# Two interleaved heads per band section instead of four, with a new order of all engines

## The chip, the cores and the metric

The kernel runs on one core of one Trainium2 chip. The metric is the device time of one execution in microseconds (us); the number to beat is the median of three executions, 129.38 us.

## The reference

Two independent layers read a sequence of 2048 positions and 448 features each, and their results stand side by side in the output (2048 x 896, bf16).

```python
# A: sliding attention, 16 heads of 28, window of 8 positions with a step of 2
qkv = (x @ wqkv).reshape(B, S, 3, H, Dh).transpose(2, 0, 3, 1, 4)
idx = pos[:, None] - (jnp.arange(8) * 2)[None, :]          # s, s-2, ..., s-14
logits = jnp.einsum("bhsd,bhswd->bhsw", q, k[:, :, idx]) * Dh ** -0.5   # idx < 0 is masked
o = jnp.einsum("bhsw,bhswd->bhsd", softmax(logits), v[:, :, idx])
a = o.transpose(0, 2, 1, 3).reshape(B, S, D) @ wo
# B: a diagonal complex recurrence of 448 states
h[t] = Lam_bar * h[t - 1] + B_bar @ x[t]
y[t] = 2 * Re(C @ h[t]) + x[t] * Dskip
```

## The kernel before, in words

**The order.** Every operation is a small function with a name, and the string `ORDER` lists the calls one by one. The position in that list is the order in which each engine receives its instructions; nothing is reordered later. A step such as `QK041@23` puts its result into PSUM banks 2 and 3; a trailing `.` lets ScalarE empty the bank and a trailing `=` lets VectorE do it. Each engine walks through its own part of the list and waits where an operand isn't ready, so a late step delays all that is behind it on the same engine.

**Layer A.** `QA`, `QK` and `V_` (lines 343 to 361 and 510 to 518) multiply x by wqkv on TensorE; `qk`, `qh` and `v` empty the banks. `P(u, r)` (line 402) is one VectorE multiplication of queries with eight shifted copies of the keys, 128 x 4096 elements; there are 14. Its result is a tile of a pool with three buffers, so the fourth `P` waits until the `E_` of the first has read it. `E_` (lines 415 and 419) sums the products over the 28 features of a head on TensorE, `lt`, `TR` and `tr` bring the logits to rows of positions, and `sma`, `smb`, `smc` are the softmax of one half u of the sequence (VectorE, ScalarE, VectorE).

The weighted sum over the window is a banded matrix product. `AL(g)` shifts the attention weights of four blocks of 64 positions into place, `al` writes them to a zeroed tile, `ad` copies that tile to DRAM, and `sp(g)` (line 505) reads it back so that each row arrives one position later than the row before it: the band `PT`. For each group of `HS` heads the band stores `HS` values of one position next to each other. `AV(B, hg, par)` (lines 531 and 537) then takes one head out of it as the moving operand, every `HS`-th element, 128 x 135 at a time; four heads run in four groups of 32 columns of the array. The lines that carry `HS`:

```python
PW = HS * (128 + 7)
SP.dma_start(late["PT"][32 * s:32 * s + 32, sl:sl + 4, :, 32 * HS * s:32 * HS * s + 39 * HS].rearrange("p t g n -> p (t g) n"),
             pd_ap(g, 32 * s * 2560, [[2560 - HS, 32], [40 * HS, 64 // HS], [1, 39 * HS]]))
PE.matmul(p[32 * hh:32 * hh + 32, 128 * bl:128 * bl + n], v_s[:, t, 4 * hg + hh, :],
          PT[:, t % NS, (4 * hg + hh) // HS, (4 * hg + hh) % HS:HS * n:HS], start=(bl == 0 and B == 0), stop=True, skip_group_check=True)
```

`AV(0, ...)` needs `sp(0)` and `sp(1)`, `AV(1, ...)` needs `sp(2)` and `sp(3)`; `sp(3)` overwrites the part of `PT` that `AV(0, ...)` reads. `av` empties the bank, `W_` multiplies by wo, `w` and `ow` bring the rows out.

**Layer B.** The recurrence is split into four phases j of 512 steps and seven groups g of 64 complex states. `BU` and `BR` build the inputs (banks emptied by `z`), `UP`, `y`, `sa`, `sb`, `sd` run the scan over 256 longer steps on VectorE (g in pairs 0, 2, 4 and 6), and `DN`, `dn` finish phase 3. The carried-in state must then be added, rotated, to phases 0 to 2 of every group: 21 rotations. A rotation goes one of two ways. `H_` and `h` (lines 790 and 795) do it as one TensorE matmul and one VectorE addition. `ha` and `hb`, or `ka` and `kb` (lines 819 and 823), do it as two VectorE instructions, once `sw(g)` has fetched a copy with the halves swapped. `C(j, ct)` multiplies the finished states of all seven groups by the output matrix, `c` adds the skip term on VectorE, `oc` writes the rows out. `CH` and `ch` are the last block in two parts.

Of the kernel before, what the change touches and what calls it, by code (L numbers as in the profile page):

```python
# [18 lines left out]
NC = S // T  # L19
N2 = NC // 2  # L20
G = 7
HS = 4
PW = HS * (128 + 7)
NS = 12
PI = math.pi
# [4 lines left out]


ORDER = """
WU@0 XI0@12 xi00. xi20= XI1@3 xi31. QA000@4 xi30= QA200@5 xi01= PP@6 pcopy pa xi21= pb QA10@7 pd_ XA11@0 XH1@1 xh1. pe
QA001 xa11= pc pf XA10@2 QA201 QA30@6 xa10= QA11@3 tf1 ts01 tf5 ts05 QA01@1 ts11 QK011 qk010. QK001 qk001. V_111@02
V_110 ts21 QA21@7 tz xt0 pg pk QA31@1 QK031 v111. QK021 qk011. QK041@23 ts15 qk021. rb2 qk031. ts25 qk020. QK040 tf0
qk041. P01 wc= qk040. rb0 qk000. qk030. QK050@71 v110. V_100@53 QK051 qk050. ts00 ts10 qk051. QK061@24 V_101 tf6
V_001@60 V_000 v101. QK060 ts20 QK110@71 ts06 ts16 xt2 v100. v000. ts26 P03 qh001. E_01@3 qh000. E_03 P05 E_05 qh010.
qh011. v001. tf3 QK100@56 P02 P00 QK101 qk100. ts03 QK111 qk110. V_011@24 qk111. qk101. V_010 v010. v011. QK130@05
QK131 V_401@71 QK121@62 P04 E_00@4 ts13 E_02 E_04 qk130. QK120 tf2 qk131. hc0 ts23 qk121. ts02 V_400 P06 v400. P10
E_06 v401. ts12 lt00 ts22 QK141@05 BD P11 V_511@27 lt01 qk120. QK140 TR0@1 xt3 xt1 V_510 tr0. qk141. E_11@4 tf4 P13  # L40
qk140. E_10@3 ts04 QK161@61 LC v510. v511. P12 QK151@50 QK150 qk150. ts14 qk151. QK160 qh100. P14 qh111. V_410@27 sma0
qh101. qh110. V_500@50 hc1 V_501 v500. V_411 v410. E_12 E_13 OZ BU201@61 v501. v411= BU301@52 BU200 P15 ts24 XR tx
smb0 BU300 z30. P16 z20. BU000@07 BR31 BR21 ci0. CD0 E_14 z31. z21. ci3. ci2. E_15 smc0 CD2 BU311@56 BU001 BU401@21
E_16 rb1 lt10 lt11 BU400 TR1@3 BU310 ci1. z40. xd2 z00. BU500@42 BR41 tr1. BR32 z32. AL0@0 BR01 CD1 al0. z01. CD3
BU010@35 BU011 BU501 z41. sma1 smb1 BU101@07 ad0 BR02 z02. BR33 z33. z50. rb3 BU100 OP pm0 z10. BU210@13 BR11 BU211
xd0 smc1 pm1 BU111@40 ca6 pm3 pm4 z11. wo BU110 BR12 ca3 BR22 z12. xd3 BR03 z22. AL1@7 cs6 BR13 AL2@4 cs3 al1. BR51
z03= sp0 UP0 BR23 xd1 z13. y0= UP1 z51. y1. sa0 AL3@1 al3. BU410@72 al2. z23. sb0 sd0 ad1 ca0 ad2 BU511@50 BU411
BU601@14 UP3 ca5 cs5 pm2 y3. BR42 sp1 UP2 z42. BU600 BU510 BR52 z60. z52. DN0@6 BU611@71 BR61 y2. cs0 BR53 z53. BR43
BU610 UP5 z43. UP4 ad3 z61. BR62 ca2 y5. sa2 AV030@5 AV010@3 av010. sp2 AV031@4 av031. AV020@0 AV000@3 AV011@4 y4.
av000. AV021@2 z62. AV001@3 av030. dn0 BR63 av020. sb2 sd2 H_20@6 sa4 W_00@7 z63. h20 sp3 W_10@5 sb4 UP6 W_30@0 av001.  # L50
av021. w00. av011. sd4 y6. DN2@3 ca4 cs4 dn2 H_11@6 W_01@2 w10. w30. ow00 W_21@7 H_01@4 DN4@1 w21. dn4 sw5 sa6 h11
W_31@5 W_11@0 H_00@7 w11. W_20@3 w31. cs2 h00 h01 sb6 ha15 H_21@1 AV111@0 AV130@5 ow11 ow10 AV101@6 w20. ow31 av111.
ow21 ca1 h21 cs1 AV131@3 sd6 sw4 AV121@0 AV120@7 av120. sw2 AV100@4 ha24 AV110@1 av100. av121. C33@7 DN6@4 dn6 av110.
av131. C31@0 ha23 av130. av101. W_60@1 W_70@3 ow30 ha22 sw3 hb15 ha26 hb24 ha25 w01. W_41@5 H_10@4 w70. C32@6 hb23
ow01 sw6 h10 W_71@2 C30@3 ha03 w60. ow60 hb25 H_12@1 W_50@4 w41. hb26 ow41 ow20 c30 W_61@5 w61. hb22 c33 ow70 ow61
ha13 ka04 ha14 W_51@3 w51. hb13 oc33 w71. ow71 hb14 w50. W_40@7 C21@5 h12 ha16 w40. hb03 C20@3 hb16 c20 c21 ow40 C22@2
oc21 H_02@4 c31 C10@7 c22 oc22 h02 C13@1 C23@3 ka06 oc30 oc31 oc20 kb04 ka05 c32 oc32 kb05 kb06 C12@5 ow50 C11@0 c11
c12 ow51 c13 c23 c10 oc11 oc12 oc13 C01@2 c01 C00@4 c00 oc23 oc10 C02@6 CH0@0 CH1@5 oc01 c02 oa00 oc02 ch0 oh0 ch1 oh1
"""

@with_exitstack
def kernel(
# [46 lines left out]
    def ps(dt=F32):  # L109
        return ps_p.tile([128, 512 if dt == F32 else 1024], dt, tag=f"ps{banks.pop(0)}", name="ps")  # L110

    def evict(e, o, i):
        (ACT.copy if e == "A" else V.tensor_copy)(o, i)  # L113
# [356 lines left out]
    def pd_ap(g, off, ap):  # L470
        p = pds[g][:]
        return bass.AP(p.tensor, p.offset + off, ap)

    @op
    def AL(g):
        p = pp["al", g] = ps()
        p4 = p.rearrange("p (t g w h) -> p t g w h", t=4, g=H // HS, w=W)

        def at(t0, n, cc):
            return attn[:, t0:t0 + n, cc:cc + H].rearrange("p t (g h) -> p t g h", h=HS)  # L480
        for w in range(W):
# [7 lines left out]
    def ak(g):  # L489
        return Ak0[:, g] if g < 2 else late["Ak"][g]  # L490

    @op
    def al(g, e):
        evict(e, ak(g).rearrange("p (s n) -> p s n", n=40 * HS)[:, :, 0:W * HS],
              pp.pop(("al", g)).rearrange("p (s n) -> p s n", n=W * HS))

# [5 lines left out]
    def sp(g):  # L502
        sl = (4 * g) % NS
        for s in range(4):
            SP.dma_start(late["PT"][32 * s:32 * s + 32, sl:sl + 4, :, 32 * HS * s:32 * HS * s + 39 * HS].rearrange("p t g n -> p (t g) n"),
                         pd_ap(g, 32 * s * 2560, [[2560 - HS, 32], [40 * HS, 64 // HS], [1, 39 * HS]]))
# [467 lines left out]
```

## Time and profile before

| | before |
|---|---|
| median of 3 runs | 129.38 us (129.23 to 130.12) |
| profiled execution | 130.03 us, its span in the profile 128.3 us |
| granted TensorE clock | 0.996 |
| TensorE matmul busy | 121.7 us (95%) |
| VectorE busy | 118.3 us (92%) |
| ScalarE busy | 90.2 us (70%) |
| DMA | 23.28 MB in 44916 packets |

The profile comes from one execution, which took 130.03 us, 0.65 us above the median; its span of 128.3 us leaves 1.7 us outside of the records. Busy times are unions over the span. [...]

### The profile page before, as it was taken

To read this page: it belongs to the slowest core of one execution; us is meant where nothing else is said; L and a number is where in the kernel's file an instruction comes from. 1 tells how busy PE (TensorE), PEld (TensorE's weight loads), DVE (VectorE), ACT (ScalarE), POOL (GpSimd) and SP (SyncE) were. 2 spreads that over 40 slices of the span, in tenths; PEclk is the share of its full clock that TensorE was granted. 3 is DMA by queue.
4 is the path that set the end of the run, shared out by engine and by line. 5 is a ranking of instruction groups with operands and counts; after the bars stand their busy time and mean duration, and the time that the engine had idled before them with its cause. 6 is when DMAs were issued, how large, how long until landed. Compare 5 with 4: busy or idle time off the path is not lost.

```text
span 128.3 us, 2859 instructions
## 1 busy us (share of the span) xinstructions
PE 121.7 (95%) x1071; PEld 61.9 (48%) x1071; DVE 118.3 (92%) x192; ACT 90.2 (70%) x184; POOL 20.0 (16%) x44
## 2 busy tenths in 40 slices
PE   6899999699999999999999999999999999999990
PEld 6663344233434434345335444955684555555550
DVE  5689999699999999999999999999999999999990
ACT  1559999969699889997999999999579404200000
POOL 6802000000000000069997000000000000000000
PEclk9999999999999999999999999999999999999998
DMA  3989979899999986995549799958264341305462
GB/s 91 338 236 254 251 186 178 190 185 284 154 211 238 209 222 211 369 197 131 205 119 193 247 287 276 208 99 156 48 181 103 97 143 40 111 0 179 138 212 80
DMA packets 44916, 23.28 MB, mean 181 GB/s; under 512 B 31143, under 2 KB 43879, under 8 KB 44903
## 3 DMA queue, kind: packets, MB, share of 16 engines
q1 hardware_dynamic: 44152, 22.71, 73.1%
q10 hardware_dynamic: 751, 0.40, 1.1%
q8 instruction: 8, 0.13, 0.4%
q14 instruction: 5, 0.04, 0.1%
HBM read 11.68 MB, written 6.29 MB: 140 GB/s over the span
## 4 chain that ended last, share of the span: by engine, by line
DVE 37%; PE 26%; SPq 12%; ACT 12%; DMA 5%; issue 4%; DVEq 0%; ACTq 0%
PE ps L854 16%; DVE pr L402 14%; SPq L169 5%; PE ps L550 5%; ACT Z L113 4%; ACT ctmp L684 3%; SPq L175 3%; DMA wq<-in_A_wqkv_dram 3%; PE ps L250 2%; DMA xT<-xbuf 2%; DVE hs L763 2%; DVE Z L795 2%; DVE R L666 2%; PE ps L415 2%; DVE xnB L844 2%
## 5 line engine op out<-in xcount | busy, mean ns | idle before, releaser
L402 DVE TENSOR_TENSOR pr<-qf,kf 128x4096 bf16<-128x4096 bf16 x12 | 27.0, 2287 | 1.4 <-PE ps L415 1.3
L250 PE MATMUL ps<-xbuf,BT 128*128 128x512 bf16 (+1 forms) x112 | 23.4, 379 | 0.0
L854 PE MATMUL ps<-Cw,Z 128*128 128x448 bf16 x105 | 20.9, 353 | 0.0
L250 PE MATMUL ps<-xT,wq 128*128 128x512 bf16 (+1 forms) x88 | 18.4, 380 | 1.3 <-DMA xT<-xbuf 1.3
L113 ACT CAST Z<-ps 128x512 bf16<-128x512 f32 (+1 forms) x33 | 15.5, 523 | 1.2 <-PE ps L722 1.1
L854 PEld LDWEIGHTS <-Z 128*128 128x128 bf16 x105 | 10.2, 98 | 9.9 <-DVE Z L770 0.3
L250 PEld LDWEIGHTS <-BT 128*128 128x128 bf16 (+1 forms) x112 | 8.8, 97 | 12.5 <-issue 3.6
L113 ACT CAST ya<-ps 128x448 bf16<-128x448 f32 (+1 forms) x17 | 8.5, 550 | 7.9 <-issue 4.7
L550 PE MATMUL ps<-wo,oT 128*128 128x448 bf16 x64 | 13.4, 352 | 0.0
L250 PE MATMUL ps<-wq,xT 128*128 128x448 bf16 (+1 forms) x64 | 12.7, 353 | 0.0
L250 PEld LDWEIGHTS <-wq 128*128 128x128 bf16 (+1 forms) x88 | 6.3, 96 | 12.5 <-issue 6.3
L931 POOL MEMSET PT<- 128x4320 f32 x3 | 11.0, 3701 | 8.0 <-DVE z L461 8.0
L113 ACT CAST oT<-ps 128x512 bf16<-128x512 f32 x17 | 9.3, 611 | 1.2 <-PE ps L537 0.9
L684 ACT ACTIVATE ctmp<-Cw,c2t 64x448 f32<-64x448 bf16 x14 | 9.3, 667 | 0.4 <-DVE attn L464 0.2
L819 DVE SCALAR_TENSOR_TENSOR Ak<-Z,co,Z 128x512 f32<-128x512 bf16 x13 | 9.4, 744 | 0.0
L823 DVE SCALAR_TENSOR_TENSOR Z<-BT,co,Ak 128x512 bf16<-128x512 bf16 x13 | 9.4, 746 | 0.0
L550 PEld LDWEIGHTS <-oT 128*128 128x128 bf16 x64 | 6.2, 98 | 5.7 <-ACT oT L113 0.2
L537 PE MATMUL ps<-PT,v_s 128*32 128x135 bf16 (+1 forms) x256 | 8.6, 300 | 0.0
L860 DVE TENSOR_TENSOR xbuf<-ps,xnB 128x448 bf16<-128x448 f32 x15 | 8.4, 616 | 0.0
L113 ACT CAST qf<-ps 128x512 bf16<-128x512 f32 x12 | 6.7, 599 | 2.2 <-PE ps L250 2.2
L250 PEld LDWEIGHTS <-xT 128*128 128x128 bf16 (+1 forms) x64 | 5.2, 97 | 6.0 <-issue 1.3
L113 ACT CAST v_s<-ps 128x448 bf16<-128x448 f32 x15 | 7.5, 541 | 0.3 <-PE ps L250 0.3
(151 smaller groups left out, 191.4 us busy)
## 6 DMA issues: line engine op xcount, KB each, us to landing
PT<-pd SPq DMA_DIRECT2D x16, 156.0 KB, 4.4
xnB<-in_B_x_dram SPq DMA_DIRECT2D x2, 896.0 KB
out_dram<-ya SPq DMA_DIRECT2D x16, 112.0 KB, 2.4
out_dram<-xbuf SPq DMA_DIRECT2D x14, 112.0 KB, 1.8
pd<-Ak SPq DMA_DIRECT2D x2, 640.0 KB
xbuf<-in_A_x_dram SPq DMA_DIRECT2D x2, 448.0 KB
xnB<-in_B_x_dram SPq DMA_DIRECT2D x4, 224.0 KB, 6.2
xnB<-in_B_x_dram SPq DMA_DIRECT2D x4, 192.0 KB, 3.6
```

Of the source, the lines that this page charges most:

```text
L113: (ACT.copy if e == "A" else V.tensor_copy)(o, i)
L169: SP.dma_start(xP[:, 2 * hh + q, :, d0:d1], xB_r[hh, :, q, :, b, c:c + d1 - d0])
L250: PE.matmul(o, l, r, start=(first and i == 0), stop=(not first and i == len(pairs) - 1 and not more[s]))
L402: V.tensor_tensor(t[:], q.unsqueeze(1).to_broadcast((128, 8, 512)), k8, ALU.mult)
L537: PE.matmul(p[32 * hh:32 * hh + 32, 128 * bl:128 * bl + n], v_s[:, t, 4 * hg + hh, :], PT[:, t % NS, (4 * hg + hh) // HS, (4 * hg + hh) % ...
L550: PE.matmul(p[:, 0:D], late["oT"][:, b // 4, hg, par, 128 * (b % 4):128 * (b % 4) + 128], late["wo"][:, hg, :], start=(hg == 0), stop=(hg ...
L684: ACT.activation(t[a:a + 64, 0:D], Cw[b:b + 64, g, :], ACTF.Copy, scale=c2t[a:a + 64, g:g + 1])
L819: e.scalar_tensor_tensor(t.rearrange("p (a n) -> p a n", a=2), prev(g), co2[:, 0, j, g:g + 1], late["Z"][:, g, j, :].rearrange("p (a n) -> ...
L823: e.scalar_tensor_tensor(late["Z"][:, g, j, :], BT[:, g].rearrange("p b n -> p (b n)"), co2[:, 1, j, g:g + 1], pp.pop(("ht", j, g)), ALU.m ...
L854: PE.matmul(p[:, 0:D], z, Cw[:, g, :], start=(g == 0), stop=(g == G - 1))
L860: V.tensor_tensor(yo, pp.pop(("c", j, ct))[:, 0:D], xnB[:, ct, j, :], ALU.add)
L931: POOL.memset(late["PT"][:, 4 * i:4 * i + 4].rearrange("p t g n -> p (t g n)").bitcast(F32), 0.0)
```

## The change

`HS` goes from 4 to 2, and `ORDER` is replaced as a whole. No function changes. The diff, with only the ends of the two lists:

```diff
-HS = 4
+HS = 2
...
 ORDER = """
-WU@0 XI0@12 xi00. xi20= XI1@3 xi31. QA000@4 xi30= QA200@5 xi01= PP@6 pcopy pa xi21= pb QA10@7 pd_ XA11@0 XH1@1 xh1. pe
...
-c12 ow51 c13 c23 c10 oc11 oc12 oc13 C01@2 c01 C00@4 c00 oc23 oc10 C02@6 CH0@0 CH1@5 oc01 c02 oa00 oc02 ch0 oh0 ch1 oh1
+WU@0 XI0@12 xi00. xi20. XI1@3 xi21= PP@4 QA200@5 xi01. QA000@6 QA30@7 XA10@0 pcopy pa pb xi30. pe xi31. XA11@1 QA001
...
+c13 oc13 C01@5 c11 ow71 c01 oc11 C00@1 c12 oc12 C02@6 ow41 c00 oa00 tx c10 oc10 CH0@0 CH1@3 c02 oc01 oc02 ch0 oh0 ch1
+oh1
 """
```

Three stretches of the new list on which the prediction leans (start, scan, second half of the attention):

```diff
+pc XH1@4 pd_ xa10= xh1= xa11. QA01@2 pf QA21@3 tf3 xt0 tf5 ts03 ts13 QA201 xt1 BD ts23 QA31@0 QK031 QK001 pg qk031=
+QK021 wc= tf2 QA10@1 ts05 QA11@4 qk021. QK011 qk030. qk001. QK041@37 QK040 QK050@02 QK051 qk000. qk010. qk020. rb2 rb0
+ts02 ts15 P03 ts12 V_011@61 qk041. qk011. P01 QK061@57 V_010 v010. QK060 v011. ts22 ts25 V_100@46 V_101 qk050. tf0
...
+z52. z62. AV001@6 av001. cs5 AV010@1 av010. AV030@5 BR53 z42. AV011@6 BR63 z63. av030. DN2@4 H_11@1 AV020@3 BR43 z43.
+z53= av011. av020. H_01@5 sp2 cs2 UP5 dn2 H_22@4 AV000@6 h01 AV031@5 av000. AV021@3 sp3 UP4 y5= av021. y4. UP6 H_20@7
...
+ow11 AV121@5 AV101@1 av101. h12 AV111@0 av121. h00 cs4 AV131@6 AV130@2 sw3 AV110@3 sa6 AV120@1 av111. sw4 av131. cs1
+AV100@5 av100. av110= ow01 w00. sb6 ow31 sd6 W_51@0 w51. h21 ha23 W_61@6 av130. av120. W_71@5 W_60@4 W_50@0 ha24
```

With HS = 2 the band keeps its size, but `sp` reads runs of 39 x 2 values (156 bytes) instead of 39 x 4 (312 bytes), twice as many of them, and `AV` steps through `PT` by 2 elements (4 bytes) instead of 4 (8 bytes).

The step lists differ as follows. Three rotations, (0, 3), (1, 3) and (2, 2), move from `ha`/`hb` to `H_`/`h`; `sw2` falls away. Bank emptying goes from VectorE to ScalarE for xi20, xi30, xi01, xa11, v411 and z03, and from ScalarE to VectorE for xh1, qk031, z01, z13, y1, z53, y5 and av110. All else is the same set of steps in another sequence.

More of the change, by code (lines that the diff above doesn't have):

```diff
@@ L32 @@
 ORDER = """
-WU@0 XI0@12 xi00. xi20= XI1@3 xi31. QA000@4 xi30= QA200@5 xi01= PP@6 pcopy pa xi21= pb QA10@7 pd_ XA11@0 XH1@1 xh1. pe
[L34 to L57, printed above, removed]
@@ new lines @@
+qk051. qh010. P00 qh011. E_01@1 v100. E_03 qk040. V_410@02 qh000. QK110@74 QK111 qh001. V_411 hc0 qk111. P05 qk110.
+v411. QK100@35 ts00 ts10 v410. QK121@47 QK120 v101. QK141@20 QK101 qk120. qk101. tf4 P02 pk E_00@6 E_05 QK140 qk140.
+P04 QK130@45 qk121. QK131 qk100. ts20 E_02 ts04 P06 qk130. E_04 xt2 xt3 qk131. tf1 QK161@27 E_06 lt01 LC lt00 QK160
+qk141. qh100. TR0@3 tr0. V_001@45 V_401@16 ts01 V_000 v000. P13 v001. V_500@03 qh111. P11 ts14 V_501 qh110. V_400
+v500. v501. QK151@45 E_11@7 E_13 XR ts11 qh101. P12 ts24 V_111@03 V_110 ts21 QK150 v110. v111. qk151. qk150. sma0
@@ new lines @@
+v400. tf6 V_511@20 V_510 ts06 v511. P10 E_10@3 smb0 hc1 E_12 P15 BU201@54 BU200 OZ P14 BU301@10 BU300 v510. v401. P16
+z30. ci3. ci2. ts16 E_15 E_14 BR31 z31. smc0 CD2 BU000@26 ci0. rb1 E_16 BU311@10 CD3 lt10 BU310 BR32 BU001 CD0 rb3
+z20. lt11 TR1@3 z32. ci1. tr1. sma1 CD1 AL0@5 xd0 BR21 z00. OP BU101@71 BU100 z10. pm0 z21. al0. BR33 BR01 BU010@32
+z01= ad0 BR11 z33. UP3 BU011 smb1 BU111@74 y3. BU110 BR02 z11. z02. BR12 z12. xd1 smc1 BU500@56 BR13 BR03 BU501 ca0
+cs0 pm3 BU401@01 z50. pm1 wo BU601@37 z03. z13= BU600 ca6 z60. UP1 BR51 UP0 AL1@5 al1. xd2 ca3 sp0 BR61 y1= y0= sa0
@@ new lines @@
+BU210@34 BU211 AL2@2 pm4 ad1 cs6 BR22 al2. ad2 z61. BU400 z22. BU611@52 BR23 sb0 xd3 z40. BR41 z23. z41. AL3@7 UP2
+al3. BU410@30 sd0 y2. BU511@17 BU510 pm2 z51. sa2 cs3 sb2 sd2 sp1 BU610 DN0@4 dn0 ca5 ca2 ad3 BR62 BR52 BU411 BR42
+z52. z62. AV001@6 av001. cs5 AV010@1 av010. AV030@5 BR53 z42. AV011@6 BR63 z63. av030. DN2@4 H_11@1 AV020@3 BR43 z43.
+z53= av011. av020. H_01@5 sp2 cs2 UP5 dn2 H_22@4 AV000@6 h01 AV031@5 av000. AV021@3 sp3 UP4 y5= av021. y4. UP6 H_20@7
+W_10@6 H_13@3 W_30@0 h11 h22 h20 ts26 sa4 sb4 av031. W_21@1 w21. w10. y6. H_02@4 ow21 ow10 h13 H_21@7 sd4 H_03@5
@@ new lines @@
+W_01@1 ca4 H_10@6 w30. h02 w01. h10 W_11@2 W_31@3 w31. ca1 W_20@0 w20. DN4@1 h03 ow30 W_00@4 H_00@3 H_12@6 dn4 w11.
+ow11 AV121@5 AV101@1 av101. h12 AV111@0 av121. h00 cs4 AV131@6 AV130@2 sw3 AV110@3 sa6 AV120@1 av111. sw4 av131. cs1
+AV100@5 av100. av110= ow01 w00. sb6 ow31 sd6 W_51@0 w51. h21 ha23 W_61@6 av130. av120. W_71@5 W_60@4 W_50@0 ha24
+W_40@3 DN6@2 dn6 ha25 hb23 sw5 C32@1 ha16 hb24 ha26 ow20 W_70@7 w60. w50. ow60 ha14 tz w70. ow00 C31@4 ow50 c32 sw6
+hb26 oc32 C33@0 C30@2 w71. c33 ow51 w61. W_41@7 oc33 hb25 C21@5 hb16 ha15 hb14 C23@6 w41. hb15 C20@1 C22@0 ow70 c31
@@ L59 @@
+c30 oc31 c21 C10@7 c20 ka06 c23 oc20 C11@4 oc23 ka04 c22 ka05 oc21 kb05 w40. oc30 ow40 kb04 C13@3 ow61 C12@2 oc22 kb06
+c13 oc13 C01@5 c11 ow71 c01 oc11 C00@1 c12 oc12 C02@6 ow41 c00 oa00 tx c10 oc10 CH0@0 CH1@3 c02 oc01 oc02 ch0 oh0 ch1
+oh1
 """
```

## The prediction

> **What bounds the kernel now.** I read the busy times first, then the same by stretches of the span.
>
> ```profile
> PE 121.7 (95%) x1071; PEld 61.9 (48%) x1071; DVE 118.3 (92%) x192; ACT 90.2 (70%) x184; POOL 20.0 (16%) x44
> ```
> ```profile
> 25.00:66.00 41.00, 40.87 (x328) 16.84 (x327) 39.27 (x38) 36.78 (x71) 10.39 (x6) 1.00 0.94 213
> 100.00:120.00 20.00, 20.00 (x107) 10.31 (x106) 20.00 (x33) 3.77 (x8) 0.00 (x0) 1.00 0.30 93
> ```
>
> The columns of the stretches are length, then busy time of PE, PEld, DVE, ACT and POOL. Two engines are full at once: TensorE idles 0.13 us of 41 and nothing of the last 20, VectorE 1.7 of 41 and nothing of 20. ScalarE has room from 100 us on. So the end moves only if both TensorE and VectorE get shorter. Next the timeline of both: where their dense stretch begins, what broke it, and where it ends.
>
> ```profile
> 4.67 0.88 DVE L113 CAST xT<-ps 128x256 bf16<-128x256 f32 x2 [0.41 <-PE ps L297]
> 14.83 2.29 DVE L402 TENSOR_TENSOR pr<-qf,kf 128x4096 bf16<-128x4096 bf16 x1
> 25.98 4.49 DVE L402 TENSOR_TENSOR pr<-qf,kf 128x4096 bf16<-128x4096 bf16 x2 [1.33 <-PE ps L415]
> 124.52 0.69 DVE L890 TENSOR_TENSOR xbuf<-ps,xnB 128x320 bf16<-128x320 f32 x2
> ```
> ```profile
> 5.07 0.62 PE L294 MATMUL ps<-ident,xbuf 128*128 128x128 bf16 x8 [0.44 <-DMA xbuf<-in_A_x_dram]
> 23.92 1.46 PE L250 MATMUL ps<-xT,wq 128*128 128x512 bf16 x6 [1.27 <-DMA xT<-xbuf]
> ```
> ```profile
> 20.79 3.00 DMA xT<-xbuf
> 112.72 0.22 PE ps L790
> 112.94 10.59 PE ps L854 x56
> 123.53 0.96 PE ps L882 x7
> ```
>
> VectorE runs from its first product P at 14.83 to 124.52 + 0.69 = 125.21 us: 110.4 us with 1.33 us in one wait, in which P02 stood for a buffer that E_01 had not read yet. The last block (chain of waits, start and length) ends on TensorE just before. From 125.21 to the end of the span are 3.1 us of output DMA and closing, which the change leaves alone. TensorE has one gate: at 23.92 it waits for the DMA transposes of the second half of x, landed at 20.79 + 3.00 = 23.79. What it does after the gate is gapless.
>
> **The change part by part.** VectorE first: rotations and emptied banks.
>
> ```profile
> 102.64 0.75 DVE L823 SCALAR_TENSOR_TENSOR Z<-BT,co,Ak 128x512 bf16<-128x512 bf16 x1
> 103.31 0.68 DVE L795 TENSOR_TENSOR Z<-ps,Z 128x512 bf16<-128x512 f32 x1
> 103.91 0.74 DVE L819 SCALAR_TENSOR_TENSOR Ak<-Z,co,Z 128x512 f32<-128x512 bf16 x1
> 104.57 0.75 DVE L823 SCALAR_TENSOR_TENSOR Z<-BT,co,Ak 128x512 bf16<-128x512 bf16 x1
> ```
> ```profile
> L113 DVE CAST Z<-ps 128x256 bf16<-128x256 f32 x2 | 0.8, 416 | 0.0
> L113 DVE CAST v_s<-ps 128x448 bf16<-128x448 f32 x1 | 0.6, 617 | 0.0
> L113 DVE CAST xT<-ps 128x256 bf16<-128x256 f32 x1 | 0.4, 425 | 0.4 <-PE ps L297 0.4
> L113 DVE COPY wq<-wq 128x512 bf16<-128x512 bf16 x1 | 0.3, 287 | 0.0
> L666 DVE TENSOR_TENSOR R<-Is,co 128x896 bf16<-128x896 bf16 x4 | 4.3, 1083 | 0.0
> L641 DVE TENSOR_SCALAR kM<-iot,fT 128x256 int32<-128x256 f32 x7 | 2.4, 347 | 0.0
> L642 DVE SCALAR_TENSOR_TENSOR fr<-iot,fT,kM 128x256 f32<-128x256 f32 x7 | 3.4, 484 | 0.6
> ```
>
> From start to start a rotation of two instructions costs 0.67 + 0.66 = 1.33 us and one by `h` 0.60. Three moved: 3 x 0.73 = 2.19 us off. A record is 0.08 longer than the distance of two starts (0.68 against 0.60), so a small bank costs VectorE 0.34, v411 0.54, and a full bank of 512 (not shown for a plain copy) about as `h`, 0.60. Behind the first P, v411 and z03 leave (0.88), z01 and av110 come (1.20) and z13, y1, z53, y5 come (1.36): 1.68 on. The step rb0 (1.0) and wc (0.2) now stand ahead of the first P: 1.2 off the dense stretch, which becomes 110.4 - 2.2 + 1.7 - 1.2 = 108.7 us if its waits stay.
>
> It starts later. VectorE has nothing to do until XI1, which starts at 5.07, is through at about 5.7, since the two banks that it emptied from 4.67 on are ScalarE's now: +1.0. Ahead of P it gains rb0, wc, xh1 and qk031 (2.1) and loses four copies of 0.35 to 0.45 (1.6): +0.5; a 0.1 of old waits goes. First P at 14.83 + 1.4 = 16.2 us.
>
> Its waits: the old 1.33 goes, since E_01 now stands ahead of the gate. The sixth product P04 takes over the buffer of P00, whose E_00 stands behind the gate and three QK blocks (3 x 1.3 plus short ones, 5.0 us, and 0.4 for itself): read at 23.9 + 5.4 = 29.3. VectorE comes there at 16.2 + 12.7 (five P of 2.2, two table steps of 0.35 + 0.48) = 28.9. A wait of 0.5 takes the place of 1.33. VectorE ends at 16.2 + 108.7 - 0.8 = 124.1 us, 1.1 earlier than before. The bounds: all small waits gone (about 1.3 more), or as many new ones again.
>
> Now TensorE: three `H_` come, 0.22 each by the chain's row of L790, +0.65. QK110, first behind the gate, has about 0.75 us more of work ahead of it than before (E_01, E_03, V_410, V_010 and V_011 in, V_110, V_111, V_000 and V_001 out: 3.4 against 2.7), so as much less stands behind. That leaves TensorE's end where it was. What decides is the AV, by how far four heads run side by side:
>
> ```profile
> 25.31 1.48 PE L415 MATMUL ps<-pr,E 128*32 128x512 bf16 x24
> 26.72 2.01 PE L250 MATMUL ps<-xT,wq 128*128 128x512 bf16 x10
> ```
> ```profile
> 79.92 4.14 PE L537 MATMUL ps<-PT,v_s 128*32 128x135 bf16 x128
> 84.00 0.39 PE L722 MATMUL ps<-Z,R 128*128 128x512 bf16 x1
> 92.51 0.20 PE L531 MATMUL ps<-PT,v_s 128*32 128x7 bf16 x4
> 92.55 0.66 PE L537 MATMUL ps<-PT,v_s 128*32 128x135 bf16 x16
> 93.02 0.21 PE L531 MATMUL ps<-PT,v_s 128*32 128x7 bf16 x4
> ```
>
> E: 24 matmuls in 26.72 - 25.31 = 1.41 us, in six groups of four: 0.235 us for 512 columns, 0.46 ns per column, operand contiguous. AV: eight in 84.00 - 79.92 = 4.08, 0.51 us each, for 4 x 133 columns: 0.96 ns per column. The second half's AV takes 0.51 too, with four short matmuls more; were weight loads the limit, 20 in place of 16 would show. The operand's step of 8 bytes is the difference left. No row has a step of 4 bytes, so the bounds are 0.51 (as now) and 0.25 (as E). [...] Saving 16 x 0.23 = 3.7 us; TensorE could end 3.7 earlier, and then it waits for VectorE.
>
> [...]
>
> The AL matmuls write runs of two values to PSUM in place of four.
>
> ```profile
> 69.97 0.19 PE L483 MATMUL ps<-attn,shf 128*128 128x64 bf16 x1
> 70.24 0.19 PE L486 MATMUL ps<-attn,shf 128*128 128x64 bf16 x1
> ```
>
> Ten of them stand 0.03 us apart, the rate of E, runs of four costing nothing. Bounds for the 60: nothing, or twice the time, +1.8 us, which the AV's saving covers. I take nothing.
>
> Last the DMA, and SP, which issues it.
>
> ```profile
> PT<-pd SPq DMA_DIRECT2D x16, 156.0 KB, 4.4
> ```
> ```profile
> 74.18 1.99 SPq L505 DMA_DIRECT2D PT<-pd  x4
> 83.86 2.44 SPq L505 DMA_DIRECT2D PT<-pd  x4
> ```
> ```profile
> DMA  8989999999999999999999999999999999965531
> ```
> ```profile
> DMA packets 3361, 0.86 MB, mean 172 GB/s; under 512 B 3360, under 2 KB 3360, under 8 KB 3360
> ```
>
> The third fence is the DMA view of 80 to 84 us, in which one set `sp(g)` of 4 x 512 packets flows: the engines are nine tenths busy for about 3.8 us, so the set is limited by them. 4096 packets of half the size cost between 3.8 (bytes decide) and 7.6 us (packets decide). The fourth is the view of 34 to 39, transposes of 256 bytes: 3360 packets in some 3 us of flow, twice that packet rate, so the rate isn't fixed. I take 5.4, the middle. [...]
>
> What covers it: sp(1) can be issued when its ad(1) has landed, 71 us, and is through by 78.5 (2.8 us earlier to issue than 74.18, with smc1 1 us earlier and ad3 behind it); AV001, the first, comes at about 78. sp(3) follows the first eight AV and lands at about 91, the second eight come at 93. Cover gone, TensorE stands, with `H_`, `W_` and `C` behind the AV.
>
> ```profile
> L113 ACT CAST oT<-ps 128x512 bf16<-128x512 f32 x17 | 9.3, 611 | 1.2 <-PE ps L537 0.9
> L646 ACT ACT_TABLE_LOAD x1 | 1.3, 1283 | 0.0
> ```
>
> ScalarE empties an AV's bank in 9.3 / 17 = 0.55 us, twice the new AV, so TensorE runs ahead of it. Of the second eight AV only the last two reuse a bank, those of av101 and av121, emptied first, 1.1 us of ScalarE behind six AV of 0.28, 1.7 us: no wait. One table load of 1.28 us moves from `tx` into smb0, where VectorE has some 9 us of other products before smc0, and ts26 brings a second one at about 86, 10 us ahead of sa6, its reader. sw2 falls from SP's queue; nothing waits for it.
>
> Sum: VectorE ends 1.1 us earlier, TensorE fits in. 129.38 - 1.1 = 128.3 us. (The profiled execution, 130.03, would give 128.9 with its 1.7 outside the span; I go by the median.)
>
> **The rivals.** A, the forecast: 126.8 to 129.2 by the bounds of VectorE's waits.
>
> B, AV stays at 0.51 us. For: no row shows a step of 4 bytes faster. Against: E's rate. TensorE then sets the end where it was, plus the waits for VectorE at DN2 and H_22, 0 to 0.6 us: 129.4 to 130.0, say 129.6. [...]
>
> C, the band arrives late, the slower side. Packets decide, 7.6 us a set; the four sets then flow back to back from 67 us on and end at 67 + 30 = 97, while the second eight AV need the last at 93. Behind them TensorE has some 30 us of work (8 AV, 6 `W_`, 15 `C`, `CH`): 97 + 30 = 127.0, 1.8 after 125.2: 131.2 us. It decides from 6.7 us a set on, (94 - 67) / 4. For: busy engines in the row. Against: the packet rate of 34 to 39 us.
>
> D, the list makes waits that I don't see: 130 to 132.
>
> **How the numbers follow.** A 0.60, B 0.18, C 0.13, D 0.09. A measurement here tells about 1% from no change, 1.3 us: faster is below 128.1, slower above 130.7. A gives faster 0.36, same 0.24; B faster 0.01, same 0.14, slower 0.03; C and D same 0.03, slower 0.19. Together 0.37, 0.41, 0.22. The range holds A and B and half of D: 126.8 to 130.6.
>
> **What would show it.** Right: eight AV of the first half in 2 to 2.5 us, not 4.08; first P at 16.2; P04 waiting about 0.5; `PT<-pd` landing in 5 to 6 us; TensorE with gaps between 80 and 110 that end on DVE. Wrong: AV still 0.51 (B), or gaps of TensorE that end on the DMA of PT (C), or VectorE's last sum not before 125.

## The result, and the profile after

| | before | after |
|---|---|---|
| median | 129.31 us (4 runs, 129.11 to 130.12) | 131.12 us (4 runs, 130.72 to 131.36) |
| profiled execution, span | 130.03 us, 128.3 us | 131.19 us, 129.5 us |
| TensorE / VectorE / ScalarE busy | 121.7 / 118.3 / 90.2 us | 121.7 / 117.9 / 92.2 us |
| DMA packets | 44916 | 52820 |

The changed kernel is slower by 1.3%, clear of the noise though small: ratio 1.0131, 95% interval 1.0086 to 1.0176. Measured again beside other kernels it took 131.34 us, 1.0172 (1.0126 to 1.0218). The forecast was 128.3 us, its range ended at 130.6.

The busy line of the page after, then four stretches of the span after and, below them, two of before (length, then busy time of PE, PEld, DVE, ACT, POOL):

```profile
PE 121.7 (94%) x1064; PEld 58.6 (45%) x1074; DVE 117.9 (91%) x191; ACT 92.2 (71%) x184; POOL 20.1 (15%) x44
```
```profile
25.00:66.00 41.00, 40.69 (x306) 15.97 (x308) 39.88 (x40) 36.63 (x70) 8.78 (x5) 1.00 0.93 214
66.00:80.00 14.00, 13.42 (x104) 6.20 (x105) 13.60 (x27) 12.17 (x23) 5.38 (x3) 1.00 1.01 193
80.00:100.00 20.00, 18.90 (x358) 10.69 (x358) 19.41 (x39) 18.63 (x38) 0.00 (x0) 1.00 0.74 126
100.00:120.00 20.00, 19.49 (x103) 9.75 (x102) 19.21 (x34) 3.98 (x9) 0.00 (x0) 1.00 0.39 118
```
```profile
66.00:80.00 14.00, 13.93 (x114) 6.51 (x116) 13.30 (x25) 13.31 (x28) 3.71 (x2) 1.00 0.97 237
80.00:100.00 20.00, 19.84 (x349) 13.49 (x350) 19.46 (x42) 16.98 (x34) 0.00 (x0) 1.00 0.64 135
```

TensorE is busy for as long as before although its AV became faster, and it now has gaps: 0.6, 1.1 and 0.5 us in the last three stretches, where it had 0.1, 0.2 and none. A second execution of the changed kernel had TensorE busy for 123.1 us, so that a busy time of a whole span is good to about 1 us. VectorE lost its full stretch behind 100 us (19.21 of 20). Next VectorE's timeline: the first P, P04, the last rotation of phase 2 with its wait, and the end.

```profile
17.04 4.49 DVE L403 TENSOR_TENSOR pr<-qf,kf 128x4096 bf16<-128x4096 bf16 x2
30.17 2.29 DVE L403 TENSOR_TENSOR pr<-qf,kf 128x4096 bf16<-128x4096 bf16 x1 [0.40 <-ACT qf L114]
108.92 0.75 DVE L824 SCALAR_TENSOR_TENSOR Z<-BT,co,Ak 128x512 bf16<-128x512 bf16 x1 [0.66 <-DMA BT<-Z]
125.70 0.69 DVE L891 TENSOR_TENSOR xbuf<-ps,xnB 128x320 bf16<-128x320 f32 x2 [0.33 <-PE ps L883]
```

VectorE ends at 126.39 us, 1.2 later than before. The row at 108.92 is hb26 (`hb` of phase 2, group 6), waiting for the swapped state of that group (`sw6`). TensorE's timeline around the AV:

```profile
85.11 0.95 PE L538 MATMUL ps<-PT,v_s 128*32 128x135 bf16 x48 [0.34 <-ACT oT L114]
85.99 0.39 PE L735 MATMUL ps<-Z,R 128*128 128x256 bf16 x2
89.30 0.36 PE L551 MATMUL ps<-wo,oT 128*128 128x448 bf16 x1 [0.41 <-ACT oT L114]
95.22 0.19 PE L532 MATMUL ps<-PT,v_s 128*32 128x7 bf16 x4
97.67 1.67 PE L551 MATMUL ps<-wo,oT 128*128 128x448 bf16 x8
```

From start to start three AV take 85.99 - 85.11 = 0.88 us, 0.29 each, and the second eight with their short pieces 97.67 - 95.22 = 2.45 us, 0.31 each: the faster AV is there. So are new waits for ScalarE's `oT`, the tile into which it empties the banks of the AV. The DMA row of PT and SP's issues (start, length; the last two are four output issues and then the first half of `sw6`):

```profile
PT<-pd SPq DMA_DIRECT2D x16, 156.0 KB, 4.9
```
```profile
73.40 4.08 SPq L506 DMA_DIRECT2D PT<-pd  x4
102.39 2.07 SPq L561 DMA_DIRECT2D out_dram<-ya  x4
104.56 0.60 SPq L814 DMA_DIRECT2D BT<-Z  x1
```

A DMA of PT lands after 4.9 us in the median (4.4 before), and the issue of a set of four keeps SP for 4.08 us (1.99 before). The experiments show that both steps of the change have a part in this. The chain that ended last (start, length):

```profile
105.22 3.58 DMA BT<-Z
110.20 0.67 DVE Z L824
110.92 13.79 PE ps L855 x72
124.71 0.96 PE ps L883 x7
```

The swap for hb26 lands at 108.8, hb26 and hb25 follow on VectorE, TensorE waits 0.48 us at C21 for hb25, and from 110.92 on it runs without a gap to the end. Before, the chain ended on TensorE too, but next to nothing had held it up behind 24 us (0.36 us of gaps in 100).

### The profile page after: what moved, and what is told of

Read it like the earlier page. It is cut to its first block, busy times and chain, and to the rows that moved or that the text cites. A ratio compares the mean times of both kernels' runs of the same rounds, so it can differ in the third digit from the quotient of the medians.

```text
span 129.5 us, 2853 instructions
## 1 busy us (share of the span) xinstructions
PE 121.7 (94%) x1064; PEld 58.6 (45%) x1074; DVE 117.9 (91%) x191; ACT 92.2 (71%) x184; POOL 20.1 (15%) x44
## 2 busy tenths in 40 slices
DMA packets 52820, 23.15 MB, mean 179 GB/s; under 512 B 39303, under 2 KB 51783, under 8 KB 52807
## 5 line engine op out<-in xcount | busy, mean ns | idle before, releaser
L251 PE MATMUL ps<-xbuf,BT 128*128 128x512 bf16 (+1 forms) x109 | 23.9, 381 | 0.3
L114 ACT CAST Z<-ps 128x512 bf16<-128x512 f32 (+1 forms) x29 | 14.4, 530 | 1.7 <-PE ps L723 1.3
L551 PE MATMUL ps<-wo,oT 128*128 128x448 bf16 x64 | 13.9, 352 | 0.4 <-ACT oT L114 0.4
L114 ACT CAST oT<-ps 128x512 bf16<-128x512 f32 x16 | 8.7, 616 | 1.1 <-PE ps L487 0.8
L114 ACT CAST v_s<-ps 128x448 bf16<-128x448 f32 x16 | 8.0, 536 | 1.5 <-PE ps L251 1.4
L824 DVE SCALAR_TENSOR_TENSOR Z<-BT,co,Ak 128x512 bf16<-128x512 bf16 x10 | 7.1, 748 | 0.7 <-DMA BT<-Z 0.7
L796 DVE TENSOR_TENSOR Z<-ps,Z 128x512 bf16<-128x512 f32 x11 | 7.2, 683 | 0.2 <-PE ps L791 0.2
```

The lines of the kernel that those rows point to most:

```text
L251: PE.matmul(o, l, r, start=(first and i == 0), stop=(not first and i == len(pairs) - 1 and not more[s]))
L551: PE.matmul(p[:, 0:D], late["oT"][:, b // 4, hg, par, 128 * (b % 4):128 * (b % 4) + 128], late["wo"][:, hg, :], start=(hg == 0), stop=(hg ...
L796: V.tensor_tensor(zz, pp.pop(("h", j, g))[:], zz, ALU.add)
L824: e.scalar_tensor_tensor(late["Z"][:, g, j, :], BT[:, g].rearrange("p b n -> p (b n)"), co2[:, 1, j, g:g + 1], pp.pop(("ht", j, g)), ALU.m ...
```

## The experiments

Each is a change to the step list, or to `HS`, of one of the two kernels; moved steps are shown as - and +, with the rest of the list left out. Times are medians; each ratio is to the kernel before, measured at the same time on the same chip, with its 95% interval. Between groups of runs the kernel before took 128.71 to 129.31 us, so ratios are compared, not times.

### Two heads alone, and the new order alone

```diff
-HS = 4        # order of before
+HS = 2
```

> The order of before with the band interleaving two heads instead of four; nothing else is changed. Theory S (TensorE's saving on AV is real, and what ate it in the changed kernel is the new order: more switches between matmul shapes): the sixteen AV go from 0.51 to 0.28 us each, TensorE's busy time falls by 3 to 3.7 us, the longer issue of the four PT reads (3.7 to 4.1 us a set instead of 1.9) is covered as before had room for it, and as VectorE sets the end in this order the time is 128.5 to 129.4 us. Rival D (the two-head band itself costs: longer issue on SP, later PT, later W and output): 130.0 to 131.2 us, with waits of TensorE on PT ahead of the AV.

129.74 us, ratio 1.0047 (1.0019 to 1.0075). TensorE's busy time fell to 118.6 us, 3.1 less than before, and nothing of it reached the end. The busy line of its page and two rows of its timeline say where it went:

```profile
PE 118.6 (93%) x1061; PEld 59.2 (46%) x1071; DVE 118.2 (92%) x192; ACT 90.0 (70%) x184; POOL 20.0 (16%) x44
```
```profile
80.32 1.07 PE L537 MATMUL ps<-PT,v_s 128*32 128x135 bf16 x56 [0.95 <-DMA PT<-pd]
95.53 0.19 PE L531 MATMUL ps<-PT,v_s 128*32 128x7 bf16 x4 [1.38 <-DVE Z L795]
```

One microsecond became a wait for PT, 1.4 us a wait for a sum on VectorE, at the last AV. VectorE is as full as before (118.2 us) and has no wait of 0.15 us or more from 94.80 us to its end; the time is above theory S's upper bound and below D's range. SP's issue of the first two sets of PT grew to 2.41 and 2.76 us only (1.90 and 1.99 before; theory S had 3.7 to 4.1), and a DMA of PT landed after 4.5 us (4.4).

```diff
-HS = 2        # order of after
+HS = 4
```

> The changed kernel with the band interleaving four heads as before; nothing else is changed. Theory S (TensorE is what sets the changed kernel's end): sixteen AV at 0.51 instead of 0.28 us are +3.7 us in a TensorE row with about 1 us of slack in this stretch, so 133.0 to 134.8 us. Rival V (VectorE's chain of late sums sets the end): the AV's time falls into TensorE's waits, 131.0 to 131.7 us. Rival D (the two-head band itself costs more than it brings): below 131 us.

133.75 us, 1.0371 (1.0341 to 1.0401), as theory S has it. The new order by itself costs 4.6 us; the two-head band gives 2.6 to 3.1 of them back, by the two ratios of the changed kernel. The busy line of this kernel's page:

```profile
PE 124.9 (95%) x1064; PEld 61.7 (47%) x1074; DVE 118.1 (89%) x191; ACT 92.6 (70%) x184; POOL 20.1 (15%) x44
```

The four kernels make a square. TensorE busy: 121.7 before, 118.6 with two heads, 124.9 with the new order, 121.7 with both. The order puts 3.1 to 3.2 us on TensorE, the band takes 3.1 to 3.2 off. Each corner is one execution, and the changed kernel's second one read 123.1, so the square is surer in kind than in its last half microsecond. Three `H_` matmuls are 0.65 of the 3.2; the other 2.5 are not in the prediction.

### What the new order puts on TensorE

In the list, the 128-row matmuls alternate with 64-row pieces (the last 64 of 448 features: the steps ending in 1 of `QK`, `V_`, `BU`) and with matmuls of 32 output rows (`E_`, AV). Counted from the lists, the kernel before changes between these shapes 39 times, the changed one 67 times. To price a change by itself, each 64-row piece of before was put right behind its own 128-row part:

```diff
-V_111@02 V_110 ... QK041@23 ... QK040 ...
+V_110@02 V_111 ... QK040@23 QK041 ...        # and so for the other pairs: 39 -> 80 changes of shape
```

> The kernel before (four heads, its own order) with each 64-row piece of QK, V_ and BU put right behind its own 128-row part, so that no two stand together: 80 switches between matmul shapes instead of 39, the same matmuls. It measures the price of a switch by itself. Theory S (0.095 us a switch, TensorE gapless): 41 more are 3.9 us, 132.5 to 133.3 us, and TensorE's busy time 125 to 126 us. If the lost time around the pieces is not the switch but the piece's own pipeline, within 0.5 us of before, 129.0 to 129.8 us.

133.91 us, 1.0374 (1.0343 to 1.0405), somewhat above theory S. Two rows of before, then two of this kernel and the busy line of its page:

```profile
41.32 3.30 PE L250 MATMUL ps<-xT,wq 64*128 64x512 bf16 x16
44.46 0.73 PE L250 MATMUL ps<-wq,xT 128*128 128x448 bf16 x3
```
```profile
42.37 3.52 PE L250 MATMUL ps<-xT,wq 128*128 128x512 bf16 x15
45.82 0.36 PE L250 MATMUL ps<-wq,xT 128*128 128x448 bf16 x1
PE 125.3 (95%) x1061; PEld 61.4 (46%) x1071; DVE 118.6 (90%) x192; ACT 90.4 (68%) x184; POOL 20.0 (15%) x44
```

Sixteen matmuls take 44.46 - 41.32 = 3.14 us where two 64-row pieces stand together, with one change of shape up to the next row. The same sixteen take 45.82 - 42.37 = 3.45 us with four changes (x15, since one record is missing: two starts lie 0.43 us apart, twice the usual distance). In the records, which overlap (0.38 us each), 128-row matmuls of 512 columns begin 0.216 us apart, and 0.31 to 0.32 apart where the shape changes: 0.095 to 0.1 us each. Over the kernel, TensorE's busy time rose by 3.6 us for 41 changes, 0.09 each; the median time rose by 4.8 us, and the rest of that is not explained here. By that price the 28 more of the changed kernel are 2.5 to 2.7 us: the gap in the square.

The traces of the two kernels themselves say the same. Behind 10 us, I took the distance of starts across each change that follows no wait and subtracted what the columns take without a change (0.216 us for 512). In before, 38 changes cost 3.7 us; in the changed kernel, 63 cost 6.2 us; the median is 0.094 and 0.096 us. The 2.4 us between them are in the changed kernel's own record.

Taking twelve of them out of the changed kernel:

```diff
-QK121@47 QK120 v101. QK141@20    +QK120@47 v101. QK121 QK141@20
-QK161@27 (behind tf1)            +QK161@27 (behind QK131)
-V_501 qh110. V_400 v500.         +qh110. V_400 V_501 v500.
-V_511@20 V_510                   +V_510@20 V_511
-BU200 OZ P14 BU301@10            +BU301@10 BU200 OZ P14
-BU001 (behind BR32)  -BU411 (behind ad3)  +BU001 (behind BU311)  +BU411 (behind BU410)
```

> The changed kernel with six of its 64-row pieces (QK121, QK161, V_501, V_511, BU301 with BU201, BU001, BU411) moved a few places to stand behind another 64-row piece: 55 switches between matmul shapes instead of 67, the same instructions otherwise. Theory S: twelve switches at 0.095 us are 1.1 us less of TensorE's row; if TensorE alone sets the end 129.9 to 130.2 us, if VectorE is close behind 130.3 to 130.7 us. Rival V (VectorE's late sums set the end): 130.9 to 131.4 us. If the pieces are not what costs, TensorE's busy time is within 0.3 us of 121.7 us.

130.98 us, 1.0170 (1.0127 to 1.0212), between the ratios of the changed kernel and its second measurement: no gain. TensorE's busy time did fall, to 120.9 us, and became waiting. Stretches of TensorE alone, changed kernel, then this one:

```profile
24.00:66.00 42.00, 41.64 (x310) 1.00 0.93 214
80.00:100.00 20.00, 18.90 (x358) 1.00 0.74 126
```
```profile
24.00:66.00 42.00, 41.13 (x312) 1.00 0.92 211
80.00:100.00 20.00, 18.58 (x356) 1.00 0.76 127
```

So the switches (changes of shape) alone do not set the end either. That VectorE stands right behind TensorE is the likely reason; this run does not show it.

### The waits at the end

First the late table load (`ts26`, the first Sin behind the softmax's Exp, has a load of 1.28 us ahead of it at 86.97 us, and `av031` and with it a `W_` stand behind it on ScalarE):

```diff
-ts16 (behind ci2)  -ts26 (behind h20)  -tz
+ts06 ts16 ts26
```

> The changed kernel with the last two steps of the angle tables (ts16, ts26) moved up behind ts06, ahead of the first Exp of the second softmax, and without tz, which would load the Sin table again: no table load among the evictions at 87 us. Theory G (VectorE's row up to hb25, the last rotation before C21, sets the end, and the load reaches it through oT, W_ and the sums h by what TensorE waits at 89.3 us, 0.36 us, and VectorE 0.1 to 0.2 us): 130.7 to 131.1 us. Theory S (TensorE's row alone sets the end): also 0.3 to 0.4 us less. Rival A (ScalarE's load is what made the changed kernel slow): 129.5 to 130.0 us.

130.89 us, 1.0146 (1.0118 to 1.0174), as theory G has it and 0.9 us above rival A's range: the load is not the cause.

Next the gate, the wait of TensorE at C21 for hb25:

```diff
-sw6 (behind ow50)  -ha16 (behind hb23)  -ha14 (behind ow60)
+sw6 (behind dn6)   +ha16 (behind hb25)  +ha14 (behind hb16)
```

> The changed kernel with three steps moved: sw6, the swap that hb26 waits for, goes right behind dn6 on SP instead of behind four output issues (0.8 us earlier), and ha16 and ha14 go behind hb25 (two passes of 0.67 us out of the way of the rotations that C21 waits for). Theory G (hb25 is the gate of the last 72 C matmuls): hb25 ends 1.3 to 2 us earlier, TensorE's 0.5 us wait at C21 goes and the time is 130.2 to 130.7 us, then bound by TensorE's row with its 67 switches. Theory S alone (TensorE only): within 0.3 us of the changed kernel.

131.65 us, 1.0213 (1.0181 to 1.0246): rather slower than the changed kernel (the intervals overlap), against both theories.

```profile
108.34 0.75 DVE L823 SCALAR_TENSOR_TENSOR Z<-BT,co,Ak 128x512 bf16<-128x512 bf16 x1 [1.61 <-DMA BT<-Z]
109.62 0.92 PE L550 MATMUL ps<-wo,oT 128*128 128x448 bf16 x4 [1.08 <-ACT ya L113]
```

The swap lands little earlier (hb26 at 108.34 instead of 108.92), since `sw5` and `sw6` now stand back to back on SP. The four output issues behind them start at 106.17 instead of 102.39, `w` on ScalarE waits for a free buffer of `ya`, its bank is not emptied, and TensorE waits 1.08 us at a `W_`. SP's queue is full here (in the changed kernel its issues follow each other within 0.1 us from 101.10 to 105.85): what was moved ahead on it made something else late. All three changes together:

> The changed kernel with all three mends: the twelve switches fewer, the tables early, and hb25 early. Theory B (TensorE's row and VectorE's gate stand at the same place, so that mending one of them shows little and both together show): 1.1 us of switches, 0.5 us of the wait at C21 and 0.3 us of the table load off TensorE's row, 129.0 to 129.7 us. Rival V (something else on VectorE sets the end): 130.3 to 131.0 us, as for each alone.

131.50 us, 1.0208 (1.0162 to 1.0255), with the same wait of TensorE for `ya`, 1.2 us. It says nothing on theory B. Then the gate without a step moved on SP, by taking rotation (2, 6) off VectorE:

```diff
-ha26 ... hb26
+H_26@2 (behind C32) ... h26 (in ha26's place)
```

> The changed kernel with one rotation more, (2,6), taken from VectorE to TensorE: ha26 and hb26 (two passes of 0.67 us, the second of which waited 0.66 us for its swap) go, one matmul of 0.22 us and one sum of 0.60 us come. No queue is reordered. Theory G (VectorE's row up to hb25 gates the last 72 C matmuls, at which TensorE waited 0.48 us): hb25 ends 1.4 us earlier, TensorE's wait there goes, and from there TensorE's row sets the end: 130.3 to 130.8 us. Theory V (VectorE's work alone sets the time): 1.4 us less, 129.6 to 129.9 us. Theory S (TensorE alone): 131.2 to 131.5 us.

130.69 us, 1.0146 (1.0113 to 1.0179): in theory G's range by the time, though the ratio lies between the two of the changed kernel. hb25 ended at 109.65 instead of 110.86 and the waits at hb26 and C21 are gone. The end of the chain:

```profile
109.98 14.57 PE ps L854 x77
124.55 0.96 PE ps L882 x7
```

TensorE runs into the last block without a gap, and yet this block starts only 0.16 us earlier (124.55, not 124.71): with VectorE's gate gone, TensorE's own work and its earlier waits set the end.

With the twelve switches and the tables on top:

> The same kernel with nine rotations on VectorE, and with the twelve shape switches fewer and the angle tables early, each of which alone was within 0.3 us of the changed kernel. Theory B (TensorE's row and VectorE's gate stand within half a microsecond of each other): with the gate out of the way the 0.8 us that the regrouping took off TensorE's busy time reach the end, and the load's 0.3 us: 129.0 to 129.8 us. If the time stays at 130.5 to 131.2 us, neither the switches nor hb25 is what is left, and the cause is another.

130.38 us, 1.0123 (1.0088 to 1.0158): the best of the new order, short of theory B's 129.8. It is 0.3 us under the run without them, where the twelve switches alone are 1.1 us by their price. From 90 us on TensorE has no gap here. And with two AV moved so that five stand together, 51 switches in all, measured beside the changed kernel itself:

```diff
-AV030@5 BR53 z42. AV011@6 BR63 z63. av030. DN2@4 H_11@1 AV020@3 BR43
+AV030@5 AV011@6 AV020@4 BR53 z42. BR63 z63. av030. DN2@3 H_11@1 BR43
```

> The changed kernel with nine rotations, 55 switches and early tables, and with two of the AV moved so that the first five stand together: 51 switches. Theory B (with the gate at hb25 gone, TensorE's row is gapless to the end and each switch is paid): 0.4 us less than with 55, 129.8 to 130.2 us, and 0.8 to 1.3 us under the changed kernel measured beside it. If it is within 0.3 us of the changed kernel, the switches are not what the end is paid in.

> The changed kernel itself, unaltered, beside the others on the same chip: 130.7 to 131.4 us. It is the mark for the version with 51 switches.

131.22 us, 1.0173 (1.0134 to 1.0212), against 131.34 us, 1.0172, for the changed kernel. What the kernel it is built on had won (1.0123) is gone, as far as the overlapping intervals tell: five AV at 0.28 us in a row run ahead of the data and of ScalarE.

```profile
80.88 0.81 PE L537 MATMUL ps<-PT,v_s 128*32 128x135 bf16 x40 [0.42 <-DMA PT<-pd]
85.31 0.38 PE L790 MATMUL ps<-Z,R 128*128 128x512 bf16 x1 [0.77 <-ACT oT L113]
```

The scattered AV of the new list cost switches and save waits; moving them together saved four switches and brought these waits.

The start, with two of the copies that had left VectorE (xi20, xi30) put back:

```diff
-xi20. XI1@3 xi21= PP@4 ... xi30.
+xi20= XI1@3 xi30= xi21= PP@4 ...
```

> The changed kernel with the two copies xi20 and xi30 on VectorE, as before, in the time in which it waits 1.7 us for its first operand; ScalarE is that much earlier at pa, for which VectorE waited 0.67 us. Theory V (the first P of the band at 17.04 instead of 14.83 us is what VectorE lost): the first P at 16.0 to 16.4 us and 0.6 to 1.0 us less, 130.1 to 130.5 us. Theory G (the time after the first P is set by what stands between, P02's and P04's waits and the gates at the end): the first P earlier, the time within 0.3 us of the changed kernel.

131.02 us, 1.0165 (1.0122 to 1.0209): no gain, and the first P did not move.

```profile
4.68 0.88 DVE L113 CAST xT<-ps 128x256 bf16<-128x256 f32 x2 [0.42 <-PE ps L297]
6.99 0.17 DVE L588 TENSOR_TENSOR are<-dt,P 128x7 f32<-128x7 f32 x1 [0.67 <-ACT dt L584]
17.05 4.49 DVE L402 TENSOR_TENSOR pr<-qf,kf 128x4096 bf16<-128x4096 bf16 x2
```

VectorE waits for `pa` (its result `dt`) until 6.99 either way; the two copies fill time in which it had nothing to do.

### The rotations in the old order

The first try at two heads and ten rotations in the order of before held output matmuls up:

```diff
-ha22 ha03 ha13 sw2 hb22 hb13 hb03        # HS = 2
+H_22@2 (behind w01) h22   +H_13@5 (behind w41) W_61@3 h13   +H_03@7 (behind c33) h03
```

> The order of before with the two-head band and with three rotations, (2,2), (1,3) and (0,3), taken from VectorE (two passes of 0.67 us each) to TensorE (a matmul of 0.22 us and one sum of 0.60 us on VectorE); sw2 falls away. It is the change's idea without its new order. Theory O (the new order is what cost the time, in switches and waits): VectorE's work falls by 2.2 us, TensorE's stays 2.5 us under before, 127.3 to 128.5 us. Rival D (the two-head band's later PT, seen as TensorE's waits of 1.0 us on PT and 1.4 us on a sum of VectorE in the two-head order of before, decides): 129.2 to 130.0 us.

131.86 us, 1.0218 (1.0184 to 1.0252). TensorE waited 0.56 us at `H_03` for the bank that `c33` empties and 0.79 us at a `W_` for a sum. The places of the new matmuls brought these waits, so the run tells little of the idea. With `H_13@4` behind C21 and `H_03@1` behind C20:

> The order of before with the two-head band and ten rotations on VectorE, as in the last such run, but with the matmuls of (1,3) and (0,3) put behind C21 and C20, where banks are free, so that no output matmul waits for their sums. Theory V (VectorE sets the end of the two-head order of before): 2.2 us of VectorE less, 127.6 to 128.4 us. Theory T (in that order some 26 us of TensorE's matmuls stand behind the last scan, sd6, gapless from 97 us to the end, so that a rotation moved to TensorE is paid there): 129.5 to 130.4 us, VectorE idle for 2 us or more between 100 and 125 us.

130.51 us, 1.0123 (1.0084 to 1.0161), just above theory T's range and far from V's. The rotations without the two-head band:

```diff
-HS = 2        # the kernel above
+HS = 4
```

> The order of before, four heads, and only the rotations of the change: (2,2), (1,3) and (0,3) go to TensorE. Theory T (TensorE's row of before is gapless from 24 us to the end): three matmuls more are 0.65 us of it, 129.4 to 130.0 us, with VectorE idle for 1.5 us or more behind 100 us. Theory V (VectorE sets the end of before): 2.2 us of VectorE less, 127.0 to 128.0 us.

129.67 us, 1.0059 (1.0032 to 1.0087), theory T. Behind 100 us:

```profile
100.00:112.00 12.00, 12.00 (x65) 6.11 (x64) 10.49 (x17) 3.87 (x8) 0.00 (x0) 1.00 0.31 97
112.00:124.00 12.00, 12.00 (x65) 6.25 (x64) 11.43 (x21) 0.00 (x0) 0.00 (x0) 1.00 0.39 124
```

VectorE is idle for 2.1 us, TensorE for nothing: what was taken off VectorE (118.3 to 116.7 us busy) became waiting, and the 0.65 us put on TensorE are paid. Last, two heads and ten rotations with VectorE's work ahead of the last scan (`sd6`) cut:

```diff
-H_00@7 H_01@4 h00 h01 ha15 (ahead of sd6)
+H_00@5 H_01@3 (behind H_02) h00 h01 (behind h02)  ha15 (ahead of hb15)
```

> The order of before, two-head band, ten rotations on VectorE as in the run before, and beside that the two sums h00 and h01 with their matmuls and ha15 (together 1.9 us of VectorE) moved from ahead of the last scan to behind it, where their results are first needed. Theory T (TensorE's 26 us of matmuls behind the last scan, sd6, set the end of the two-head order of before, so sd6 is what has to come earlier): sd6 ends near 95.7 instead of 97.8 us, TensorE's wait ahead of the last AV goes, and 1.0 to 1.6 us less than the 130.5 us without it: 128.6 to 129.6 us. Theory V (VectorE's total sets the end): no change, 130.2 to 130.8 us.

130.12 us, 1.0078 (1.0047 to 1.0108). sd6 ended at 95.15 us, earlier than theory T asked, but the ratio fell by 0.0045 only (0.6 us), to a time between the two theories, and stays above before. The busy times of both engines are lower than before in this kernel, and still it is slower:

```profile
PE 118.8 (93%) x1064; PEld 59.5 (47%) x1074; DVE 116.6 (91%) x189; ACT 89.9 (70%) x184; POOL 20.0 (16%) x44
```
```profile
111.81 0.60 PE L790 MATMUL ps<-Z,R 128*128 128x512 bf16 x2 [0.81 <-DVE xbuf L860]
107.95 0.69 DVE L795 TENSOR_TENSOR Z<-ps,Z 128x512 bf16<-128x512 f32 x1 [0.76 <-PE ps L790]
```

The two engines wait for each other here, 0.81 and 0.76 us in these two rows, and TensorE waits 1.1 us for PT elsewhere. No version made here beats the kernel before.

## Why the prediction was wrong, by its own steps

**What bounds the kernel: right, and not enough.** Both engines are full, so that the end moves only if both get shorter. The two single runs show it: 3.1 us off TensorE alone, and 1.6 us off VectorE's busy time alone, ended at 1.005 and 1.006 of the time before. But both shorter did not move it either: the last run has 2.9 us off TensorE and 1.7 off VectorE, and ends at 1.008. The forecast let VectorE's gain pass to the end whole; in that run, waits of the two engines for each other and for PT took it.

**AV: right.** 0.28 was taken, 0.29 to 0.31 measured; the band alone took 3.1 us off TensorE. Rival B fell: four matmuls side by side took 0.51 us an AV at a step of 8 bytes and 0.29 to 0.31 at 4. The 0.28 was the author's estimate between two bounds, 0.51 (as before) and 0.25 (as E), and no row of before shows it; the saving of 3.7 us worked out from it no run shows: the band alone brought those 3.1. Why the shorter step is faster was not shown.

**"TensorE fits in": the step that failed.** Its terms were the AV, the `H_` and 0.75 us moved ahead of the gate. The changes of shape were put at nothing without a word, and they were in the list: 28 more at 0.095 us, 2.4 us in the changed kernel's trace. Measured, TensorE's busy time is 121.7 us as before (123.1 in the second execution). The forecast had taken TensorE out of the question, and with it every wait that VectorE has for it. The price stood in the prediction's own rows: of the 26.72 - 25.31 = 1.41 us of the six groups of four E, the last group, ahead of the next shape, takes 0.32 in the trace, the others 0.22 each. The gaps of TensorE between 80 and 100 us end on ScalarE (0.25, 0.34 and 0.41 us), not on VectorE as forecast: the prediction saw that ScalarE empties a bank more slowly (0.55 us) than an AV fills it (0.28, its estimate), and worked that out for the second eight AV, not for the first.

**VectorE's work: right to a few tenths, with some luck.** Forecast without waits: 108.7 - 1.33 = 107.4 us from the first P on. Measured: 126.39 - 17.04 = 109.35, less the waits of 0.40 (P04), 0.66 (hb26) and 0.24 + 0.17 + 0.17 + 0.33 = 0.91 (the last sums, for TensorE): 107.4. Its busy time from the first P on fell by 1.2 us (106.7 to 105.4), not by the 1.7 of the sum, and smaller waits made up the difference.

**Its start: 0.84 late.** First P at 17.04, not 16.2. The +1.0 for the missing copies was wrong, since `are` starts at 6.99 in the changed kernel and at 7.02 before; the +0.5 for the work ahead of P was too, because two of the copies subtracted had stood in idle time. Part of the 0.84 can be the execution: in other traces with this start the first P stands between 16.6 and 17.1 us, once at 18.3. P04 waited 0.40 where 0.5 was forecast, but for ScalarE's `qf`, not for `E_00`: the size was luck.

**Its waits: the rest.** 0.84 + 0.66 + 0.91 and 0.1 less at P04 are 2.3 us, 126.4 instead of 124.1. hb26's wait is a queue that was passed over: the prediction saw that sw2 leaves SP, not that four output issues (2.07 us) stand ahead of sw6. The time itself was missed by 2.8 us. The other 0.5 come from the profiled executions: that of before lay 0.65 us above its median, this one 0.07.

**DMA: right in size.** 4.9 us to landing, just under the 5 to 6 forecast; rival C did not happen, though in some versions of the new order TensorE waits 0.2 to 0.5 us for PT. That SP's own issue would take longer, 4.08 us instead of 1.99, was not in it, and SP's outputs begin at 90.30 instead of 86.41. Not all of it comes from the shorter runs: with four heads the new order issued the same set in 2.62 us, and with two heads the old order in 2.76.

**The table load: reader named, queue not.** `ts26` was compared with sa6, which reads it; what stands behind it on ScalarE, `av031`, held TensorE up for 0.41 us. That cost little at the end, as the run with early tables shows.

Rival D, a list that makes waits not seen, came true in time, though part of it was no wait but more work. What stays open is how the loss splits between the switches and the waits. With the gate, the tables and twelve switches out of the way the new order is still at 1.012, TensorE without a gap from 90 us on. Taking switches out has not been shown to bring their price back at the end: twelve fewer brought 0.3 us or nothing, and four more taken out brought waits. A version of the new order with no more than 39 switches was not made.

## What to carry to other kernels

Count the changes of matmul shape in a step list before and after, as one counts instructions: at 0.1 us each the 28 more here took 2.4 of the 3.1 us that the AV had saved. No idle time shows them, since a matmul's record (0.38 us for 512 columns) is longer than the 0.31 us to the next start; only the distance of starts does. Where two engines are full, a gain on one only became its waiting here. Cutting both in different places did not help either; what each waits for from the other has to be followed through the list. An edit that moves a step ahead on a queue must be read with everything that the queue holds at that moment.

## What was not expected of the hardware

A change between 128-row, 64-row and 32-row-output matmuls cost TensorE about 0.1 us (at 512 columns, starts 0.31 instead of 0.216 us apart; median of all changes 0.094 and 0.096 us in the two traces). An AV, four matmuls side by side, took 0.28 to 0.31 us with its moving operand at a step of 4 bytes, and 0.51 at 8 bytes. Halving the runs of a DMA from 312 to 156 bytes moved its landing from 4.4 to 4.5 us in the old order and SP's time to issue four from 1.99 to 2.76 us; in the new order it moved them from 3.6 to 4.9 and from 2.62 to 4.08 us.
